# A delta-rule attention and expert kernel in a new line: joins on four quadrants, loads paced by products, first expert slots from 12 tiles

## The chip, the cores and the metric

One Trainium2 chip, one of its cores. The time is the device time of one execution in microseconds (us). The kernel before takes 500.79 us, the median of three runs (498.42 to 501.11). The change is large, so what a comparison can tell apart is far below what is at stake.

## The reference

Two parts. First a recurrence with a delta rule over 768 positions, for 4 batches of 8 heads with 48 columns; then a layer of 8 experts, of which each of the 3072 tokens takes one.

```python
k_n = k / (norm(k) + 1e-6); state = zeros(B, H, D, D)
for t in range(S):
    y[t]  = q[t] @ state
    v_old = state^T k_n[t]
    state = state + beta[t] * outer(k_n[t], v[t] - v_old)
x = y as [3072, 384]                       # token x (head, column)
logits = x @ w_gate + modality_bias[modality_id]
e = argmax(logits); gate = softmax(logits)[e]
out = gate * (relu(x @ w1[e]) @ w2[e])     # D 384, F 1024
```

## The kernel before

The recurrence is cut into 12 chunks of 64 positions. Inside a chunk the rule is a triangular system: the Gram matrix of the keys (`g`, function `gram`), scaled by beta, has to be inverted for every head. The 12 chunks are inverted in six sets of two, set 0 and 1 first. The inverse of a 64 x 64 triangle is put together: VectorE (DVE) solves small diagonal triangles column by column (`sub0_0` to `sub0_14`, lines 265 to 271, 16 x 16 for sets 0 and 1; `subx`, 32 x 32 for the others), and TensorE (PE) joins them. For sets 0 and 1 the joins of 16 to 32 are `jy`, `ya`, `jx`, `r1` (lines 289 to 302), one of each for each step i of 0 to 7: `jy` multiplies with the Gram blocks, `ya` scales the result, `jx` multiplies with the other triangle, `r1` adds it in. `wt`, `mva`, `mvb`, `mt` then lay the triangles out as R and its transpose RTB. The joins of 32 to 64 are `y1`, `ys`, `r`, `rc` (lines 375 to 389), for all 24 steps. For sets 2 to 5 the inverses travel through DRAM: `gd` writes Gram blocks, `la` reads them as rows, `rd` and `re` write the solved blocks and their transposes (made by `rt`), `rl` reads them into R and RTB.

The recurrence then runs in 24 steps i, two for a chunk (the two halves of the batch-head pairs, which alternate): `ks` (keys by state, PE), `rh` (DVE), `z` (inverse by right-hand side, PE), `zt` (eviction), `ds` (state update, PE), `sb` (eviction of the state), and beside them `pg`/`pe` (masked query-key products), `qs` and `pz` (the output y), `xo` (its eviction), `xd` (its store), `xt`/`xs` (transposes for the router) and, for each four steps, `lg`/`le`/`lt` (logits). All of it is a list of named tasks (`Plan`); the string `ORDER` (lines 28 to 49) gives their sequence, and each engine works its tasks in that sequence. SP issues the loads: `kqk`/`kq`/`ke` (keys and queries), `kv`, and it is one queue in order. `FILL` (lines 51 and 52) puts 33 matmuls of 128 x 128 by 128 columns, whose results nobody reads, ahead of named tasks (line 496).

When the logits of the first `C.tA` = 16 tiles of 128 tokens are there, `part_a` (tasks `pa`) fills the first `C.SA` = 2 slots of 512 tokens of one expert each. Their tokens are gathered (`xg`), transposed (`xp`), split into a high and a low part (`xh`, `xl`), and the first 4 of 8 blocks of the first slot's first product (`la_0` to `la_3`, three pieces each) are tasks of the attention plan. `part_b` does the same for all other tokens when the last logits are there. Behind the plan come the rest of the units (5 of 512 tokens, 2 of 256, one of at most 32), layer 1 at line 835 and layer 2 at line 926, and `out` is written by indirect scatters from GpSimd (POOL, line 930), in an order that the framework's scheduler makes.

## Time and profile before

| | us |
|---|---|
| median of three runs (lowest, highest) | 500.79 (498.42, 501.11) |
| the profiled execution | 503.82 |
| its span, first to last instruction | 502.0 |
| PE busy in it | 454.1 (90%) |
| DVE busy | 322.0 (64%) |
| ACT (ScalarE) busy | 215.0 (43%) |
| POOL busy | 132.9 (26%) |
| mean granted clock of PE | 0.908 of full |

How to read it: the shares are means over stages that differ. The first 85 us hold the Gram products, the first solver and the joins; the recurrence's steps run from there to about 260 us, with the solver of the later sets beside them; the experts take the rest. A matmul of float32 operands shows as two records of PE, so that 8 matmuls are 16 records. The granted clock is given as a share of 2.4 GHz; 0.50 is 1.2 GHz. "Idle before" a row is the time for which the engine stood still ahead of it, with what ended it; `issue` means that the profile shows no reason.

### The profile page before, as it was taken

To read this page: it belongs to the slowest core of one execution; us is meant where nothing else is said; L and a number is where in the kernel's file an instruction comes from. 1 tells how busy PE (TensorE), PEld (TensorE's weight loads), DVE (VectorE), ACT (ScalarE), POOL (GpSimd) and SP (SyncE) were. 2 spreads that over 40 slices of the span, in tenths; PEclk is the share of its full clock that TensorE was granted. 3 is DMA by queue.
4 is the path that set the end of the run, shared out by engine and by line. 5 is a ranking of instruction groups with operands and counts; after the bars stand their busy time and mean duration, and the time that the engine had idled before them with its cause. 6 is when DMAs were issued, how large, how long until landed. Compare 5 with 4: busy or idle time off the path is not lost. (4 is left out here: it accounts for less than half of the span.)

```text
span 502.0 us, 15898 instructions
## 1 busy us (share of the span) xinstructions
PE 454.1 (90%) x6661; PEld 405.2 (81%) x6661; DVE 322.0 (64%) x716; ACT 215.0 (43%) x471; POOL 132.9 (26%) x179
## 2 busy tenths in 40 slices
PE   6566999899899798998979999996999999999994
PEld 6456998787788687888768888895889889899983
DVE  3897798687789666786476887634345355345720
ACT  3623745786366351562454325213333334324520
POOL 9000613953633411101401012046103212001111
PEclk9555555999999998999898999998999999999998
DMA  8465503579477775876355516235415525239600
GB/s 291 167 142 154 172 3 89 140 190 320 133 196 191 191 228 152 231 194 181 114 172 186 194 63 190 63 108 187 140 55 166 181 73 183 80 101 359 187 20 34
DMA packets 81264, 78.07 MB, mean 156 GB/s; under 512 B 48009, under 2 KB 71568, under 8 KB 79904
## 3 DMA queue, kind: packets, MB, share of 16 engines
q1 hardware_dynamic: 78048, 67.49, 45.5%
q0 software_dynamic: 3136, 9.49, 5.6%
q8 instruction: 54, 0.88, 0.7%
q14 instruction: 26, 0.21, 0.1%
HBM read 62.27 MB, written 14.73 MB: 153 GB/s over the span
## 5 line engine op out<-in xcount | busy, mean ns | idle before, releaser
L926 PE MATMUL opb<-w2hb,h 128*128 128x384 f32 x192 | 53.0, 341 | 0.5 <-DVE oob L929 0.5
L841 DVE SCALAR_TENSOR_TENSOR h<-hpb,h 128x512 fp32r<-128x512 f32 x24 | 16.6, 692 | 44.1 <-ACT h L839 44.1
L835 PE MATMUL hpb<-xh,w1xb 128*128 128x512 f32 x144 | 41.9, 403 | 0.0
L926 PEld LDWEIGHTS opb<-w2hb,h 128*128 128x128 f32 x192 | 34.8, 188 | 1.8 <-DVE oob L929 1.0
L839 ACT ACTIVATE h<-hpb 128x512 fp32r<-128x512 f32 x24 | 14.3, 598 | 51.2 <-PE hpb L835 51.2
L926 PE MATMUL opa<-w2ha,h 128*128 128x384 f32 x128 | 34.6, 341 | 0.0
L332 POOL TENSOR_TENSOR tmx<-T,A 128x168 f32<-128x168 f32 (+13 forms) x27 | 20.5, 759 | 46.7 <-DVE T L333 45.3
L926 PE MATMUL opb<-w2lb,h 128*128 128x384 f32 x96 | 32.5, 338 | 0.0
L835 PEld LDWEIGHTS hpb<-xh,w1xb 128*128 128x128 f32 x144 | 27.4, 193 | 4.9
L416 DVE TENSOR_TENSOR RHS<-vv,ks 64x384 f32<-64x384 f32 x44 | 24.3, 552 | 6.5 <-PE ks L414 5.1
L930 POOL DMA_INDIRECT out_dram<-oob,sidxb x12 | 12.3, 1027 | 57.4 <-DVE oob L929 22.5
L178 PE MATMUL gp<-ke 48*64 48x64 f32 x576 | 17.7, 293 | 10.1 <-issue 4.5
L25 ACT COPY Sb<-S 48x192 f32<-48x192 f32 x58 | 18.1, 313 | 20.3 <-PE S L426 10.1
L795 POOL DMA_INDIRECT xgb<-xd,gidxb x12 | 12.5, 1045 | 49.2 <-DVE sidxb L707 24.0
L178 PEld LDWEIGHTS gp<-ke 48*64 48x64 f32 x576 | 15.6, 199 | 12.1 <-issue 7.7
L391 POOL TENSOR_TENSOR vv<-vv,RR 128x384 f32<-128x384 f32 x15 | 12.3, 836 | 48.8 <-DMA vv<-in_kv_dram 33.5
L926 PEld LDWEIGHTS opa<-w2ha,h 128*128 128x128 f32 x128 | 23.2, 188 | 0.8
L437 PE MATMUL y<-ZT,pb 128*64 128x96 f32 x384 | 23.1, 268 | 0.7 <-DVE ZT L26 0.5
L178 PE MATMUL gp<-kqr 48*64 48x64 f32 x896 | 18.2, 231 | 5.1 <-ACT gk L25 2.9
L333 POOL TENSOR_TENSOR T<-T,tmx 128x168 f32<-128x168 f32 (+13 forms) x27 | 22.1, 817 | 2.1
L414 PE MATMUL ks<-Sb,kqr 112*64 112x96 f32 x352 | 20.5, 255 | 1.9 <-issue 1.0
L25 ACT COPY R<-A 32x128 f32<-32x128 f32 x60 | 17.7, 296 | 10.2 <-DVE A L302 6.4
(340 smaller groups left out, 1169.9 us busy)
## 6 DMA issues: line engine op xcount, KB each, us to landing
kqr<-in_kq_dram SPq DMA_DIRECT2D x10, 1024.0 KB, 7.0
ke<-in_kq_dram SPq DMA_DIRECT2D x10, 512.0 KB
vv<-in_kv_dram SPq DMA_DIRECT2D x12, 384.0 KB, 5.4
xd<-xo SPq DMA_DIRECT2D x24, 192.0 KB, 2.8
w1rb<-in_moe_w_dram SPq DMA_DIRECT2D x12, 384.0 KB
w2rb<-in_moe_w_dram SPq DMA_DIRECT2D x12, 384.0 KB, 3.2
kk<-in_kv_dram SPq DMA_DIRECT2D x11, 384.0 KB, 6.5
w1ra<-in_moe_w_dram SPq DMA_DIRECT2D x8, 384.0 KB
```

Source lines behind the costliest of these rows:

```text
L25: if n=="scalar": nc.scalar.copy(o,i)
L178: s.I[f"g{c}"]=mm(t[p][64*h:64*h+64,64*(4*g+j):64*(4*g+j)+64],l,s.KQ[c][u:u+48,g,x,1] if a else l,start=True,stop=True)
L332: E[s.e].tensor_tensor(o,T[:,:,lo:lo+na,c:c+1].to_broadcast([128,n,na,nb]),X[:,:,c:c+1,c+1:32].to_broadcast([128,n,na,nb]),ALU.mult)
L333: x=T[:,:,lo:lo+na,c+1:32]; E[s.e].tensor_tensor(x,x,o,ALU.subtract)
L414: for p in range(2): mm(s.ks[i][64*p:64*p+64,:,j,:],s.KQ[c][:,g,4*p+j,0],hc(s.Sb[g][:,4*p+j,:]),start=True,stop=True)
L416: c,g=divmod(i,2); b=64*p; V.tensor_tensor(s.RHS[g][b:b+64,:,48*p:48*p+48].rearrange("q (h j) c -> q h j c",h=2),s.KV[c,1][b:b+64,g],s.ks[ ...
L437: for p in range(2): mm(s.y[i][64*p:64*p+64,:,j,:],s.PB[i//2][:,8*(i%2)+4*p+j],hc(s.ZT[i%2][:,4*p+j,:]),start=(i<2 and j==0),stop=True,ski ...
L795: s.nc.gpsimd.indirect_dma_start(xg,None,S["x"],bass.IndirectOffsetOnAxis(ap=S["gidx"][:,S["c0"]+t:S["c0"]+t+1].bitcast(U32),axis=0))
L835: if n in ks: mm=s.nc.tensor.matmul(hp[:,v,:],w[:,k,fs],x[:,k,0:T],start=(n==0),stop=(n==8))
L839: if k==0: s.nc.scalar.activation(hh,hp,AF.Relu)
L841: s.nc.vector.scalar_tensor_tensor(hl,hp,0.0,hh.bitcast(F32),ALU.max,ALU.subtract)
L926: mm=nc.tensor.matmul(op,h[:,f%nf,ts_],w[:,f%2,:],start=(n==0),stop=(n==23)); n+=1
```

## The change

The plan, its tasks and its order are replaced by those of a later line of the same kernel.

- **Joins.** `jy` and `jx` of steps 0 to 7 write to two PSUM banks, and four consecutive matmuls go to the four 64 x 64 quadrants of the array, not to the two on the diagonal. `wx` lays out the second operand for that. `y1` and `r` use 32 x 32 tiles for steps 0 to 7, and 64 x 64 quadrants with half of `r`'s matmuls for the others. R is laid out by whole-width copies (`mva`, `mvb`); RTB, `mt`, `rt` and `re` are gone, a transpose by DVE (`wt`) and, for steps 8 to 23, a copy `rq` are there instead.
- **Diagonal blocks of sets 0 and 1** come into D by masked whole-width instructions (`da`, `dc`), not by 32-partition copies; `norm` is split so that the part that only later steps need (`nr0`) is a task of its own; `fin0` is halved.
- **Fillers.** `FILL` is gone. In its place stand tasks `hf7` to `hf14` (2 x 128 columns, each waiting for one solver step), `hg0`, `hg1` (3 x 128) and `hx0` to `hx19` (2 x 128, no wait).
- **Loads.** `kq` and `kv` are loaded in halves and without the empty partitions 112 to 127. Each load of the kinds kq, ke, kv, wq, wr, la and rd and each store xd waits, by a semaphore, for the PE instruction that precedes it in the order.
- **Routing.** `C.tA` is 12; `part_a` starts when three groups of logits are there. `wq3`, `wr0`, `wr1` (a fourth block of w1 and two of w2) are loaded within the plan.
- **PSUM** banks are fixed tiles that the plan hands out itself. The scatters go to four disjoint views of `out`. In the last layer 2 all matmuls of a tile come behind those of the tile before (`fl` = 0).

The new ORDER sequences 1007 tasks (916 before). The core of the diff:

```diff
-    fl=4; tA=16; TA=512; SA=2; SB=3; SC=2; SE=1; FE=32; A1=2; A2=4; wr=4; xgb=4; w_q="sync"; wlp=(); wlq=(0,1,2,3)
+    fl=0; tA=12; TA=512; SA=2; SB=3; SC=2; SE=1; FE=32; A1=2; A2=4; wr=4; xgb=4; w_q="sync"; wlp=(); wlq=(0,1,2,3)
...
-            add(f"kq{c}","SP",.9,lambda c=c: gate("g3",lambda: kq(c,slice(1024,2048))),[f"kqk{c}","g3"],mb=.39)
+            add(f"kq{c}_1","SP",.4,lambda c=c: gate("g3",lambda: kq(c,slice(1024,2048))),[f"kqk{c}","g3"],mb=.52)
...
+                            p,h=(e,f) if a else (f,e); u=64*(h^p); x=4*p+j; l=s.KQ[c][u:u+48,g,x,0] if a else s.KE[c][u:u+48,g,x]
...
-        def dc(c,p):
+        def dx(c,h): x=16*h+8*(c%2); return s.D[:,c//2,x:x+8],s.gp[c][h].rearrange("q (x t) -> q x t",x=8)
+        def da(c,h): d,g=dx(c,h); mul(d,g[:,:,32:64],s.hm[:,1:2])
+        def dc(c,h): d,g=dx(c,h); V.scalar_tensor_tensor(d,g[:,:,0:32],s.hm[:,0:1],d,ALU.mult,ALU.add)
...
+        def idle(n,k=None):
+            def f(): mm(s.bk["y"][:,0:128*n],s.ident,s.ident.unsqueeze(1).to_broadcast([128,n,128]),start=False,stop=True,skip_group_check=True)
+            gate(k,f) if k else f()
+        fy=["gf1","gf5"]; fills=[f"hf{c}" for c in range(7,15)]+["hg0","hg1"]+[f"hx{n}" for n in range(20)]
+        for c in range(7,15): add(f"hf{c}","PE",.85,lambda c=c: idle(2,f"sub0_{c}"),[f"sub0_{c}",*fy])
+        for n,k in enumerate(("fin0_0","ft0")): add(f"hg{n}","PE",1.3,lambda k=k: idle(3,k),[k,*fy])
+        for n in range(20): add(f"hx{n}","PE",.43,lambda: idle(2),fy)
...
+                jt=lambda i: s.JO[(0,1,0,1,2,2,2,2)[i]]
                 def jy(i):
-                    if i%2==0: s.jo[i]=s.jo[i+1]=s.bank(f"jo{i}",("z","ks")[i//2]) if i<4 else s.mo(f"jo{i}")
+                    s.jo[i]=jt(i)
                     for j in range(4):
-                        for p in range(2):
-                            for h in range(2): q=64*h; x=4*p+j; o=256*(i%2)+32*x; mm(s.jo[i][q:q+64,o:o+32],s.GK[i][q:q+64,x],s.W1b[i//4][q:q+64,16*p+4*(i%4)+j],start=True,stop=True)
+                        for h in range(2):
+                            for p in range(2): q=64*p; mm(s.jo[i][p][64*(p^h):64*(p^h)+64,32*j:32*j+32],s.GK[i][q:q+64,2*j+h],s.W1b[i//4][q:q+64,16*h+4*(i%4)+j],start=True,stop=True)
...
+                                k=p^h; q=64*k; n=4*(i%4)+j; w=s.Wx[i//4][q:q+64,n] if h else s.W0[i//4][q:q+64,n]
+                                mm(s.jo[i][k][64*p:64*p+64,16*j:16*j+16],s.ya[q:q+64,i%2,p,j],w,start=True,stop=True)
...
+        def rq(i):
+            r=s.R[i%4].rearrange("q (j h) t -> q j h t",h=2)[:,:,:,32:64]
+            for p in range(2): b=64*p; cp(s.e,r[b:b+32,:,1],r[b+32:b+64,:,0])
...
+            t=s.pa.tile([128,8,32],F32,name=f"Wt{i}",tag="Wt",bufs=3); s.nc.vector.transpose(t,s.R[i%4][:,:,0:32]); s.Wt[i]=t.rearrange("q (j h) t -> q j h t",h=2)
...
+        end=plan.chain("pa",lambda dry: (R.mute() if dry else R).part_a(*(((Mute(),)*3,)+(Mute(),)*4 if dry else (s.places,s.sea,s.prt(),s.mo,tp))),["lt2","y1_11","rk","rk3"],prio=900)
...
+            if s.pe and t["eng"]=="SP" and t["mb"]>.1 and t["name"][:2] in ("kq","ke","kv","wq","wr","la","rd","xd"):
+                i=next(i for i in new if "DMA" in type(i).__name__); s.tc.add_manual_dep(i,s.pe.name,mybir.DependencyInfo(mybir.DependencyClass.Sync,mybir.DependencyReason.DATA),reason="pace")
+            if t["eng"]=="PE" and new: s.pe=new[-1]
...
+        s.tc=tc; s.nc=tc.nc; s.outs=dram_disjoint_views(out,4); s.ident=ident
+        s.n+=1; return s.outs[s.n%4]
-            sc=nc.gpsimd.indirect_dma_start(s.out,bass.IndirectOffsetOnAxis(ap=sidx[:,c:c+1].bitcast(U32),axis=0),oo,None,bounds_check=3071,oob_is_err=False)
+            sc=nc.gpsimd.indirect_dma_start(s.to(),bass.IndirectOffsetOnAxis(ap=sidx[:,c:c+1].bitcast(U32),axis=0),oo,None,bounds_check=3071,oob_is_err=False)
...
```

The order of PE's tasks about the joins, after:

```
g1 g0 g3 g2 g4 g5 pg0 hx5 hx0 hx15 hx8 hx7 g6 scl1 g7 hx17 hx1 hf8 hx4 hf12 hx14 g8 hx9 hx12
hg0 hx16 jy0 jy1 hf7 jx0 hx6 jx1 hf14 jy2 scl0 hg1 hf10 jy4 jx2 hx10 y1_0 hx11 jy3 jx4 hx13 r0
hx19 jy5 jx3 hf13 hf11 scl2 jx5 hx18 hf9 jy6 hx2 y1_1 jx6 z0 r1 hx3 jy7 ds0 y1_2 jx7 qs0 z1 pz0
g10 r2 ds1 ks2 qs1 y1_3 g9 pz1 r3 z2
```

and before:

```
g1 g0 g2 g3 g4 pg0 scl1 scl0 g5 g6 g7 g8 jy0 jy2 jy3 jx0 jy1 jx2 jx1 jy4 y1_0 jx3 r0 jx4 jy5 jy6
scl2 jy7 jx5 z0 jx6 jx7 y1_1 qs0 r1 ds0 g10 pz0 ks2 z1 qs1 g9 y1_2 g11 r2 ds1 pz1 y1_3 z2
```

(FILL adds 3 matmuls ahead of pz0, 4 ahead of ks2, 3 ahead of y1_2 and 6 ahead of g11, and 17 more behind z2.) At the end of the plan, after: `... z22 pg11 r23 ks23 lg4 qs22 la_0_0 la_0_1 xt21 la_0_2 la_1_0 la_1_1 pz22 la_1_2 z23 la_2_0 qs23 la_2_1 la_2_2 pz23 la_3_0 xt22 la_3_1 xt23 la_3_2 lg5`; before: `... z23 xp3 lg4 pz23 xt21 xt22 xt23 la_0_0 ... la_3_2 lg5`.

## Rows read from the trace of the kernel before

**Rows 1.** Page, part 2: busy tenths in 40 slices of 12.55 us
```profile
PE   6566999899899798998979999996999999999994
...
PEclk9555555999999998999898999998999999999998
...
DMA  8465503579477775876355516235415525239600
```

**Rows 2.** Windows of 10 us: PE, PEld, DVE, ACT, POOL busy, PEclk, DMA share, GB/s
```profile
50.00:60.00 10.00, 10.00 (x200) 9.66 (x197) 7.40 (x17) 7.01 (x23) 6.77 (x12) 0.50 0.60 168
...
60.00:70.00 10.00, 10.00 (x182) 9.83 (x182) 8.49 (x23) 7.58 (x25) 2.65 (x5) 0.50 0.13 49
...
80.00:90.00 10.00, 9.92 (x167) 8.66 (x160) 7.71 (x12) 4.63 (x14) 2.42 (x4) 0.71 0.53 152
```

**Rows 3.** Timeline of PE, 0:95 (start us, us, engine line op out<-in xcount)
```profile
28.43 1.97 PE L178 MATMUL gp<-ke 48*64 48x64 f32 x60 [0.77 <-DVE pb L187]
...
41.61 5.33 PE L293 MATMUL jo<-w1b,gk 64*64 64x32 f32 x96 [3.38 <-DVE w1b L139]
...
58.98 1.06 PE L386 MATMUL lv<-R,ys 32*32 32x32 f32 x32
```

**Rows 4.** Timeline of PE from 80 us on: fillers (L496), products, Gram products
```profile
80.47 1.65 PE L496 MATMUL S<-ident 128*128 128x128 f32 x6
...
83.53 2.08 PE L496 MATMUL S<-ident 128*128 128x128 f32 x8
...
86.36 0.83 PE L420 MATMUL z<-RHS,R 128*64 128x96 f32 x16
...
89.65 1.60 PE L496 MATMUL S<-ident 128*128 128x128 f32 x12
...
96.20 0.88 PE L420 MATMUL z<-RHS,R 128*64 128x96 f32 x16
...
97.67 0.69 PE L386 MATMUL lv<-R,ys 32*32 32x32 f32 x32
...
101.75 1.16 PE L178 MATMUL gp<-kqr 48*64 48x64 f32 x64
...
104.46 0.49 PE L496 MATMUL S<-ident 128*128 128x128 f32 x2
...
104.88 0.88 PE L437 MATMUL y<-ZT,pb 128*64 128x96 f32 x16
```

**Rows 5.** Timeline of DVE, 0:50
```profile
8.06 1.72 DVE L26 COPY D<-gp 32x256 f32<-32x256 f32 x4 [5.81 <-PE gp L178]
...
16.71 0.48 DVE L234 MEMSET S<- 128x512 f32 x1 [0.85 <-ACT gk L25]
...
25.24 0.22 DVE L269 TENSOR_TENSOR tm<-T,A 128x60 f32<-128x60 f32 x1
...
37.96 1.23 DVE L274 TENSOR_TENSOR T<-T,t 128x1024 f32<-128x1024 f32 x1
```

**Rows 6.** Groups by line and form (xcount | busy us, mean ns | idle before)
```profile
L187 DVE TENSOR_TENSOR pb<-gp,cst 128x256 f32<-128x256 f32 x48 | 17.3, 417 | 3.3 <-PE gp L178 3.0
```

**Rows 7.** Timeline of PE: idle before a row, in brackets
```profile
14.68 1.86 PE L178 MATMUL gp<-ke 48*64 48x64 f32 x57 [4.46 <-issue]
...
165.62 0.88 PE L414 MATMUL ks<-Sb,kqr 112*64 112x96 f32 x16 [0.87 <-DMA kqr<-in_kq_dram]
...
173.12 0.25 PE L386 MATMUL lv<-R,ys 32*32 32x32 f32 x5 [2.84 <-issue]
```

**Rows 8.** Timeline of PE: last z, last piece la_3 of the first expert
```profile
256.42 0.83 PE L420 MATMUL z<-RHS,R 128*64 128x96 f32 x16
...
273.99 0.86 PE L835 MATMUL hp<-xh,w1xa 128*128 128x512 f32 x3
```

**Rows 9.** Page, part 6: KB each, median us from issue to landing
```profile
kqr<-in_kq_dram SPq DMA_DIRECT2D x10, 1024.0 KB, 7.0
```

**Rows 10.** Timeline of POOL at the end: the last scatter
```profile
496.72 0.98 POOL L930 DMA_INDIRECT out_dram<-ooc,sidxb  x1 [2.40 <-DMA out_dram<-ooc,sidxb]
```

More of the change, by code (lines that the diff above doesn't have):

```diff
@@ L306, in mv @@
-                def mv(i,p):
-                    W=w0(s.Wn[i//4],i)[:,p]; Rv=s.R[i%4].rearrange("q (j h) t -> q j h t",h=2)
-                    for h in range(2):
-                        for b in (1,0):
-                            o=64*p+32*b; q=64*h+32*b; cp(s.e,Rv[o:o+32,:,h,32*b:32*b+32],W[q:q+32])
-                MV=dict(ACT=(1.25,0),DVE=(1.0,1),POOL=(1.6,1))
-                def mt(i):
-                    for h in range(2): q=64*h; cp(s.e,s.RTB[i%2][q:q+32,:,32*h:32*h+32],s.Wt[i][q:q+32])
@@ L577, in tasks @@
         if i==3:
[L578 to L579 removed]
+            p.add(f"lg{u}","PE",.7,lg,[f"xs{4*u+j}" for j in range(4)]+["rk0"],prio=c+2,take=dict(mo=1))
+            p.add(f"le{u}","ACT",.27,le,[f"lg{u}",f"lt{u-1}" if u else None],prio=c+2,give=dict(mo=1))
             p.add(f"lt{u}","DVE",.35,lt,[f"le{u}"],prio=c+2)
@@ L967, in tile_kernel @@
     with after(PE_,A.load.ins):
-        for l,q in [(1,3)]+[(2,q) for q in range(4)]: X.load(S,l,q)
+        for q in (2,3): X.load(S,2,q)
         for q in (2,3): X.split(S["W"][1],q)
```

367 lines of the change are left out of this document (202 added, 165 removed).

## Prediction

> **What bounds the kernel now.** I read the page's slices first. TensorE (PE) is busy nine tenths or more in most slices, while its granted clock stands at half in slices 2 to 7 and at full before and after [rows 1]. So there are two kernels: up to about 85 us one at 1.2 GHz, after it one at 2.4 GHz that PE fills. The 10 us windows say what the slow stretch is: from 50 to 70 us PE is busy 10.00 of 10 and VectorE (DVE) 7.4 to 8.5, and the clock is 0.50 all the same; it comes back inside 80:90 [rows 2]. The timeline of PE gives the content: from 41.61 us on, the joins (jy, jx) of the first eight steps, 16 groups of 32 matmul records. Ninety-six records take 5.33 us, 56 ns each, although each is only 64 x 64 by 32 columns [rows 3]. A Gram product of the same clock, whose four matmuls in a row go to four different quadrants, needs 1.97 us for 60 records, 33 ns each [rows 3]. Joins before use only the two diagonal quadrants. The clock rises after the filler matmuls of 128 x 128 at 80.47 and 83.53; the second product of the recurrence (z1) starts at 86.36, still at the foot of the rise, and z2 at 96.20 [rows 4].
>
> From z2 to the last z (256.42) it is 160 us for 21 steps, with PE rarely idle: the recurrence is held by PE's own stream [rows 1, 8]. Then come the experts; their slices of PE are nines almost to the end [rows 1].
>
> **The change part by part.** The sum is made on the profiled execution (503.82 us, its span 502.0); the median of the timed runs is 500.79, so 3 us go off at the end.
>
> *Up to the first join.* DVE sets this stretch: it starts at 8.06 and reaches the first solver step at 25.24, 17.2 us with one idle gap of 0.85 [rows 5]. Four groups of quarter copies at 1.72 (one is shown) are 6.9; in their place come 12 masked instructions of 128 x 256 on DVE (4 da, 8 dc), like the masks of pb at 417 ns [rows 6], 5.0. One more eviction costs some 0.6, the two memsets of 0.48 go behind r1_3, and the idle gap, a wait for ScalarE (ACT), should go as ACT copies less: 1.9 - 0.6 + 1.0 + 0.8 = 3.1. Splitting fin0 (1.23) brings the first half's transposes 0.6 forward [rows 5]. So the first join starts near 38 instead of 41.61; bounds: nothing (a new wait for a Gram product) and 4.
>
> *Joins on quadrants, and the clock.* The 512 join records at 56 ns are 28.4 us of PE. On four quadrants they should run at the Gram price: 33 ns at half clock (16.9), or 18 ns at full, from 1.16 us for 64 records [rows 4], 9.3. The price of the records is certain to lie between 56 and 18; I take 18 because of the fillers. The change takes out 33 fillers of 128 columns, all behind the joins, and puts 20 (hx) and 8 (hf) of 256 columns and 2 (hg) of 384 ahead of and between them. Five hx in a row follow pg0, where PE otherwise waits for masks and evictions: they are hidden there, and they are as dense as the two groups of fillers before which the clock was half and after which it was full [rows 4]. Between first join and z1, 15 fillers lie on the path. At full clock twelve filler records take 1.60 us (at 89.65) [rows 4], a filler of two records 0.27 and one of 256 columns 0.53; a filler alone took 0.42 from start to start, 0.15 more than its share of a run (104.46 to 104.88) [rows 4]. So 14 x 0.68 + 0.95 = 10.5. Add five groups y1 and r at 0.69, z0 and ds0 at 0.85 each at most [rows 4], a small selection: 5.4. From first join to z1: 9.3 + 10.5 + 5.4 = 25, so z1 at 63 and not 86.36. DVE's list from the first join to z0 holds 17 steps; by the same steps of before I estimate 17 us, so it runs beside PE's 22. From z1 to z2 nine fillers (2.4 us) go, which leaves 7 to 8 of 9.8: z2 near 71, **25 us earlier**. If the clock stayed low: rival 1.
>
> Here a rule of the Trainium skill speaks against the fillers: "TensorEngine Tiling (Array Packing)", Key Properties, has it that changing the tiling mode drains the engine, and every filler between joins changes it twice. The trace agrees in kind, with the 0.15 above, which the sum holds already; without it z1 would come 2.1 us sooner.
>
> *Small joins of the later steps, transfers.* y1 and r of steps 8 to 23 go to 64 x 64 quadrants, r with half the matmuls: between nothing and 0.3 us a step, 0 to 5; I take 3. On DVE a transpose (wtr) and a copy (rq, mostly on ACT and POOL) of some 0.45 each per step are added; ScalarE's rt and the RTB and RE transfers go. Seventeen fillers behind z2 go: 17 x 0.3 = 5. Against it, seven of the 12 pieces la of the first expert product, some 0.7 each, now lie before z23 (5), and DVE, whose 19 steps from z0 to z2 I estimate at 14 us by the same steps of before, is longer there than PE: 2 more. From z2 to z23 thus 159 instead of 160.
>
> *Loads behind products.* Every large load on SP now waits for the PE instruction ahead of it in the order. Behind such a wait stand the small transfers of the same queue: rl (inverse blocks), gd, xd; for these wait wtr, y1, and the xo ring. By the new order the half loads of kq are issued 5 to 19 us of PE work before their first user; a whole kqr load of twice the size landed in 7.0 [rows 9]. I cost it at nothing, hidden by those products; where cover is thin (kq7_0, kq9_1, kv10_0, 5 to 6 us) it may cost 1 to 2 us each. The gain side: PE's idle times that end for no shown reason, 4.46 and 2.84 us, and the one wait for kqr, 0.87 [rows 7], stand in or just behind slices whose transfer engines are at seven or eight tenths [rows 1]; with bursts spread they may shrink. That is 0 to 8; I take nothing.
>
> *From z23 to the last la piece.* Before: 256.42 to 274.8, 18.4 us [rows 8]. Left behind z23 in the new order are one qs and one pz group, two transposes and five la pieces of 0.7, with z23 itself 7 to 8 us: **10 us earlier**. This is what routing from 12 tiles buys: the expert's tokens are gathered before the last products. Its weights' loads move too (w1's fourth, w2's first two).
>
> *Experts and end.* The same units (five of 512 rows, two of 256, one small) at the same matmuls: nothing, give or take 5 for another interleaving. Scatters to four views of the output no longer wait for each other's landing; the last one waited 2.40 [rows 10]. Between nothing and that is to be had, by when the last eviction ends; I take 1.4.
>
> Sum: 25 + 1 + 10 + 1.4 = 37; 503.8 - 37.4 = 466.4 for a profiled run, 463 on the median's scale.
>
> **The rivals.** *1. The clock stays at 1.2 GHz through the joins.* For it: PE was busy 10.00 at 0.50 for 20 us and more [rows 2], so being busy is not enough. By the Trainium skill, "TensorE: Matmul & The Clock Gate", What's actually happening, activity releases the throttle; the trace doesn't bear that out for the joins. Against it: dense 128 x 128 work preceded the rise [rows 4]. Price: six filler records at half clock took 1.65 [rows 4], so 1.1 for 256 columns. Joins 16.9, fillers 17, the rest 9, and the first join near 47, as the ten fillers between g7 and it no longer fit: z1 at 89 or 90, 3 later than before. Risen then, 12 us of gain remain: about 489. *1b, the slower side:* no filler is left behind z1. If the clock rises only past some 110 us, the recurrence itself runs at half clock (a group of r took 1.06 against 0.69 at full [rows 3, 4]), 10 us lost in each 25, and the 12 us won elsewhere are gone: 505 or more.
>
> *2. DVE or SP becomes the bound of the recurrence.* DVE is at 7.7 to 8.5 of 10 where PE is at half clock [rows 2]; with PE twice as fast the solver's steps for sets 2 to 5 may end late, and y1_8 waits; or the paced loads come 1 us late in ten chunks. 10 to 15 us: 475.
>
> *3. The idle times without reason go too* and DVE keeps up: 8 to 15 us more gain, 450.
>
> *4. Quadrants don't overlap for 16 and 32 columns:* up to 38 ns more a record, 19 us: 482. The Gram rows speak against it.
>
> **How the numbers follow.** Forecast (455 to 474) 0.52; rival 3 0.13; rivals 2 and 4 0.17; rival 1 0.10; 1b 0.05, and loads late by over 3.8 us in each of ten chunks, which would also end above 500, 0.03. The range 444 to 486 leaves out rival 1, both slower cases and the edge of 3, two in ten. Faster by over 0.5% (about what a measurement here tells from no change): 0.90; within it 0.02; slower 0.08.
>
> **What would show it.** The clock's slices reach full by the third or fourth; the joins at about 18 ns a record; z1 near 63, z2 near 71, z23 near 230; la pieces ending near 237; no wait of a scatter for a scatter. Wrong, if PE waits for kqr or for R's transfers in each chunk, if DVE's slices stand at nine while PE's fall, or if the clock is still half at 60 us.

## The result, and the profile after

The changed kernel takes 486.42 us (median of 4 runs, 484.85 to 496.68) beside 500.95 for the one before (4 runs): a ratio of 0.970, 95% interval 0.964 to 0.977. It is faster, as forecast, but by 14.5 us where 37 were forecast, and the time lies just outside the range. Some executions of either kernel, here the one of 496.68, are over 1.5% above its fastest, and the ratios and their intervals leave them out. The profiled execution took 487.58 (span 485.7), 16.2 less than 503.82.

First the slices of the page after, the ones that answer to [rows 1].

```profile
PE   6689888967999899899997999995999999999994
...
PEclk9589997995999999798998999997999999999999
...
DMA  5776655754667566564677234156326325239601
```

A slice is 12.1 us. The clock is back by the fourth, where before it was half up to the seventh. But it falls again, to 7, 5 and 7 tenths in slices 7, 10 and 17, and PE has a 6 and a 7 in slices 9 and 10, where [rows 1] has nines. So the early part did most of what was forecast and something later gave part of it back. The windows cut at the products z tell where (columns as in [rows 2]): from z2, z5, z8, z17, z18 and z23 of the changed kernel, and to the end of the last la piece and of the span.

```profile
76.63:96.62 19.99, 19.79 (x541) 17.88 (x539) 14.98 (x28) 12.63 (x34) 9.30 (x10) 0.83 0.64 169
96.62:130.87 34.25, 27.26 (x664) 24.49 (x658) 28.00 (x50) 13.96 (x42) 21.12 (x27) 0.80 0.53 153
130.87:191.52 60.65, 56.81 (x1391) 50.30 (x1388) 50.10 (x120) 42.58 (x127) 32.84 (x40) 1.00 0.63 174
191.52:205.56 14.04, 11.19 (x198) 10.39 (x193) 6.77 (x20) 4.62 (x15) 2.20 (x4) 0.76 0.59 172
205.56:245.20 39.64, 38.32 (x722) 32.59 (x721) 27.09 (x64) 18.59 (x52) 6.11 (x7) 0.96 0.57 160
245.20:256.44 11.24, 11.24 (x91) 8.84 (x90) 7.50 (x11) 5.69 (x9) 0.00 (x0) 1.00 0.74 235
256.44:485.70 229.26, 212.75 (x1209) 191.65 (x1209) 117.74 (x250) 75.14 (x121) 48.21 (x45) 0.97 0.42 133
```

And three stretches of the kernel before, from its z5 to z8, z8 to z17 and z17 to z18:

```profile
120.98:142.00 21.02, 19.66 (x560) 17.09 (x559) 15.77 (x37) 11.02 (x30) 9.06 (x12) 1.00 0.61 153
142.00:212.10 70.10, 63.85 (x1580) 55.55 (x1574) 51.52 (x110) 33.78 (x82) 19.56 (x24) 0.95 0.74 207
212.10:217.25 5.15, 4.86 (x133) 4.42 (x129) 4.81 (x17) 3.01 (x9) 0.00 (x0) 1.00 0.36 68
```

| stretch | before, us | after, us | difference | forecast |
|---|---|---|---|---|
| start to z2 | 96.20 | 76.63 | -19.6 | -25 |
| z2 to z5 | 24.8 | 20.0 | -4.8 | |
| z5 to z8 | 21.0 | 34.3 | +13.2 | |
| z8 to z17 | 70.1 | 60.7 | -9.5 | |
| z17 to z18 | 5.2 | 14.0 | +8.9 | |
| z18 to z23 | 39.2 | 39.6 | +0.5 | z2 to z23: -1 |
| z23 to last la | 18.4 | 11.2 | -7.2 | -10 |
| last la to the end | 227.2 | 229.3 | +2.1 | -1.4 |

A stretch does not hold the same work in both kernels, since the order is another: TensorE has 664 records from z5 to z8 where it had 560, 198 where it had 133 from z17 to z18, and 1391 where it had 1580 from z8 to z17. So a part of these three differences is work that stands elsewhere now. The rest is waits and half clock.

Two stretches stand out. From z5 to z8 VectorE has 28.0 us of work where before it had 15.8, PE is idle for 7 of 34 us and the clock is 0.80. From z17 to z18 PE is idle for 2.9 of 14 and the clock is 0.76. The timeline of PE names the waits (columns as in [rows 3], the idle time before a row and its releaser in brackets):

```profile
38.56 0.24 PE L315 MATMUL z<-w1b,gk 64*64 64x32 f32 x1
...
39.05 0.65 PE L315 MATMUL S<-w1b,gk 64*64 64x32 f32 x32
...
64.62 0.88 PE L467 MATMUL z<-RHS,R 128*64 128x96 f32 x16
...
67.61 0.49 PE L484 MATMUL y<-ZT,pb 128*64 128x96 f32 x6 [1.62 <-issue]
...
76.14 0.56 PE L426 MATMUL gp<-R,ys 32*32 32x32 f32 x23 [1.36 <-issue]
76.63 0.88 PE L467 MATMUL z<-RHS,R 128*64 128x96 f32 x16
77.44 1.50 PE L188 MATMUL MO<-ke 48*64 48x64 f32 x64
...
112.59 1.55 PE L467 MATMUL z<-RHS,R 128*64 128x96 f32 x16 [5.44 <-DVE RHS L463]
...
193.51 0.88 PE L461 MATMUL ks<-Sb,kqr 112*64 112x96 f32 x16 [0.57 <-DMA kqr<-in_kq_dram]
...
197.32 1.85 PE L188 MATMUL MO<-kqr 48*64 48x64 f32 x64 [2.27 <-DMA kqr<-in_kq_dram]
```

First join (38.56), a join group at 20 ns a record (0.65 for 32; 56 in [rows 3]) and z1 (64.62; 86.36 in [rows 4]) are as forecast. Behind three of these waits, at 76.14, 112.59 and 197.32, the same instructions run at half clock for a while (1.50 and 1.85 for 64 Gram records, 1.16 at full [rows 4]); behind the one at 67.61 the clock stays up. What VectorE did ahead of and in the 5.44 us (same columns):

```profile
97.61 0.94 DVE L259 TENSOR_TENSOR tt<-tt,A 128x64 f32<-128x64 f32 x1
...
102.60 0.55 DVE L437 TENSOR_TENSOR vv<-vv,RR 128x384 f32<-128x384 f32 x1
103.07 2.35 DVE L269 TENSOR_TENSOR A<-A,t 128x1024 f32<-128x1024 f32 x2
105.34 1.42 DVE L356 TENSOR_TENSOR tmx<-T,A 128x216 f32<-128x216 f32 x1
106.79 1.31 DVE L357 TENSOR_TENSOR T<-T,tmx 128x216 f32<-128x216 f32 x1
...
109.56 0.56 DVE L463 TENSOR_TENSOR RHS<-vv,ks 64x384 f32<-64x384 f32 x1
```

Step 6's differences (L463) stand in its queue behind the scaling of the third set (L269) and the last steps of the second elimination (L356, L357). Before the change that elimination's last step was at 102.60 us, between z3 and z4; after, it is at 110.15, between z5 and z6: the recurrence had caught up with it.

VectorE's instructions also take longer there. The norm's 0.94 (L259) is 0.27 in the kernel before, where GpSimd did nothing at the time:

```profile
114.13 0.27 DVE L243 TENSOR_TENSOR tt<-tt,A 128x64 f32<-128x64 f32 x1
```

Five such instructions of the norm and the step of 1.42 and 1.31 make some 5 of the 12 us that VectorE has more, an estimate from the durations of the same forms beside an idle GpSimd. No run takes this part by itself.

### The profile page after: what moved, and what is told of

The parts are those of the page before. It is cut to its first block, busy times and chain, and to the rows that moved or that the text cites. A ratio compares the mean times of both kernels' runs of the same rounds, so it can differ in the third digit from the quotient of the medians.

```text
span 485.7 us, 15721 instructions
## 1 busy us (share of the span) xinstructions
PE 438.1 (90%) x6567; PEld 386.7 (80%) x6567; DVE 313.0 (64%) x684; ACT 206.4 (43%) x488; POOL 154.1 (32%) x197
## 4 chain that ended last, share of the span: by engine, by line
PE 68%; DVE 14%; DMA 7%; issue 4%; ACT 2%; POOL 2%; SPq 1%; another core or an unknown queue 1%; POOLq 0%; DVEq 0%; ACTq 0%
PE hpb L889 11%; PE opb L980 9%; PE opa L980 6%; PE hpa L889 5%; PE hpc L889 4%; PE opc L980 3%; PE MO L188 3%; PE z L467 3%; PE S L473 3%; PE ks L461 3%; PE y L481 2%; PE y L484 2%; DMA w1ra<-in_moe_w_dram 2%; DVE tmx L356 2%; DVE T L357 1%
## 5 line engine op out<-in xcount | busy, mean ns | idle before, releaser
L356 POOL TENSOR_TENSOR tmx<-T,A 128x440 f32<-128x440 f32 (+14 forms) x31 | 26.6, 859 | 32.8 <-DVE T L357 31.3
L980 PE MATMUL opb<-w2lb,h 128*128 128x384 f32 x96 | 32.3, 336 | 0.0
L26 ACT COPY Sb<-S 48x192 f32<-48x192 f32 x70 | 21.9, 313 | 19.9 <-PE S L473 14.2
L463 DVE TENSOR_TENSOR RHS<-vv,ks 64x384 f32<-64x384 f32 x44 | 24.2, 550 | 9.5 <-PE ks L461 8.6
L357 POOL TENSOR_TENSOR T<-T,tmx 128x440 f32<-128x440 f32 (+14 forms) x31 | 27.8, 896 | 2.4
L467 PE MATMUL z<-RHS,R 128*64 128x96 f32 x384 | 22.2, 261 | 5.6 <-DVE RHS L463 5.6
L188 PE MATMUL MO<-kqr 48*64 48x64 f32 x832 | 19.3, 245 | 6.9 <-DMA kqr<-in_kq_dram 4.7
L26 ACT COPY ZT<-z 64x384 f32<-64x384 f32 x35 | 16.5, 472 | 20.0 <-PE z L467 19.2
L26 ACT COPY R<-gp 32x128 f32<-32x128 f32 (+1 forms) x72 | 20.2, 280 | 9.7 <-PE gp L426 5.9
L467 PEld LDWEIGHTS z<-RHS,R 128*64 128x64 f32 x384 | 18.0, 144 | 7.4 <-DVE RHS L463 6.1
L188 PEld LDWEIGHTS MO<-kqr 48*64 48x64 f32 x832 | 16.8, 156 | 8.9 <-ACT gk L26 2.6
L461 PE MATMUL ks<-Sb,kqr 112*64 112x96 f32 x352 | 21.9, 266 | 1.6 <-ACT Sb L26 0.7
```

What stands on the lines that cost most here:

```text
L26: if n=="scalar": nc.scalar.copy(o,i)
L188: s.I[f"g{c}"]=mm(t[e][64*f:64*f+64,64*(4*g+j):64*(4*g+j)+64],l,s.KQ[c][u:u+48,g,x,1] if a else l,start=True,stop=True).ins
L356: E[s.e].tensor_tensor(o,T[:,:,lo:lo+na,c:c+1].to_broadcast([128,n,na,nb]),X[:,:,c:c+1,c+1:32].to_broadcast([128,n,na,nb]),ALU.mult)
L357: x=T[:,:,lo:lo+na,c+1:32]; E[s.e].tensor_tensor(x,x,o,ALU.subtract)
L461: for p in range(2): mm(s.ks[i][64*p:64*p+64,:,j,:],s.KQ[c][:,g,4*p+j,0],hc(s.Sb[g][:,4*p+j,:]),start=True,stop=True)
L463: c,g=divmod(i,2); b=64*p; V.tensor_tensor(s.RHS[g][b:b+64,:,48*p:48*p+48].rearrange("q (h j) c -> q h j c",h=2),s.KV[c,1][b:b+64,g],s.ks[ ...
```

## The experiments

Times are ratios to the kernel before on the same chip. The changed kernel was measured twice, 0.970 (0.964 to 0.977) and 0.964 (0.957 to 0.972), so differences of less than 0.7% between two measurements say nothing. Executions of the same instructions also differ: ten profiles of kernels whose TensorE instructions don't differ before z2 (one lacks steps of an elimination) have it at 76.6 to 81.4, mean 79.6, and the changed kernel's own is the earliest.

**The early stretch: quadrants, clock or loads?** Without the fillers:

```diff
-def f(): mm(s.bk["y"][:,0:128*n],s.ident,...)
+def f(): return
```

> The 30 filler products ahead of z of step 0 are left out (20 bare ones, 8 behind steps of the first elimination, 2 behind its end). Theory C (the early gain is mostly the clock that they bring back): the granted clock stays at 1.2 GHz from 24 us until z of step 1 or 2, a group of 32 join products takes 1.3 us instead of 0.65 and a group of 64 Gram products 1.97 instead of 1.16, z of step 2 comes 12 to 20 us later (89 to 97 instead of 76.6), the kernel takes 497 to 507. Rival Q (the quadrants carry the gain, and the joins wait for VectorE anyway): z of step 2 by 82, the kernel within 5 us of 486.

Measured: 0.977 (0.969 to 0.985), z2 at 80.0. The clock is half through the joins (windows of 10 us), yet in the timeline of PE a group of 32 takes 1.08, against 1.89 for the old form at that clock:

```profile
40.00:50.00 10.00, 9.02 (x300) 8.62 (x304) 8.47 (x17) 7.64 (x26) 5.53 (x9) 0.50 0.66 192
50.00:60.00 10.00, 5.88 (x192) 5.34 (x185) 7.91 (x22) 3.21 (x13) 7.54 (x11) 0.50 0.59 176
```

```profile
46.42 1.08 PE L315 MATMUL MO<-w1b,gk 64*64 64x32 f32 x32
...
54.76 1.08 PE L315 MATMUL MO<-w1b,gk 64*64 64x32 f32 x32 [2.60 <-DVE A L331]
```

Theory C fell, Q held: the gain does not need the fillers, and the quadrants shorten the joins without them. How much of the gain they carry no run shows, as none takes the quadrants away alone, and without the loads' tie (below) most of it goes with the quadrants in place. At half clock PE is busy only 5.9 of 10 from 50 to 60 and waits for VectorE, so the clock has little to add: nothing at z2 (the ten profiles have 79.6 in the mean), and in the time 0.7 to 1.3%, which the intervals don't tell from nothing.

The reverse, the clock without the quadrants, twice. The kernel before, with fillers ahead of and between its joins (task:count, the tasks by their names):

```diff
-FILL="444:3 ... 559:1"
+FILL="444:3 ... 559:1 g6:20 g8:10 jy0:12 jy2:4 jx0:6 jy1:4 jx2:4 jx1:4 jy4:4 jx3:4 jx4:4"
```

> The kernel before, its joins not on quadrants, with 76 more products of the identity with itself (128x128) on TensorE ahead of and between its Gram products and joins from 25 us on, as many as the changed kernel has there, 20 of them ahead of the 7th chunk's Gram product. Theory C (the clock is what the early gain needs: at 2.4 GHz the old joins take half as long): the granted clock is back at 2.4 GHz by 35 us and stays, 32 join products take 0.95 to 1 us instead of 1.9, z of step 1 comes at 68 to 76 instead of 86.4, and the kernel takes 483 to 492. Rival Q (the form of the joins carries it: products of 64 rows that don't run beside one another leave the clock low however busy TensorE is): the clock falls back to 1.2 GHz inside the joins, z of step 1 at 84 or later, the kernel at 498 or more.

Measured: 0.992 (0.983 to 1.001), z1 at 85.0. The clock held to 70, a group took 1.11, and the fillers between the groups (1.16 a piece) took the room. That decides nothing, so next only 26 of them, all ahead of the joins:

```diff
+FILL="444:3 ... 559:1 g6:16 g8:6 jy0:4"
```

> The kernel before with 26 more products of the identity only ahead of its joins (16 ahead of the 7th chunk's Gram product, 6 and 4 where TensorE waited 2.7 and 3.4 us before 36 and 42), none between them. In the run with 76 the clock stood at 2.4 GHz from 32 to 68, the old joins took 1.11 us a group of 32 instead of 1.9, and the products between them took the room back. Theory C (the clock alone gives the old joins what the new ones have): the first join group starts at 41 to 43, the clock holds through the joins, 16 groups take about 18 us instead of 30, z of step 1 comes at 70 to 77 instead of 86.4, and the kernel gains 8 to 15 us. Rival Q (without work between them the old joins let the clock fall, or VectorE's chain behind them takes the time): z of step 1 at 82 or later and the kernel within 4 us of before.

Measured: 0.989 (0.982 to 0.996), z1 at 81.1, between the two expectations. Windows and timeline of PE:

```profile
40.00:50.00 10.00, 7.99 (x233) 7.70 (x232) 8.97 (x20) 6.08 (x14) 3.21 (x8) 0.94 0.82 210
50.00:60.00 10.00, 10.00 (x200) 9.66 (x197) 8.40 (x22) 7.94 (x26) 7.07 (x11) 0.50 0.65 204
```

```profile
46.47 1.12 PE L293 MATMUL jo<-w1b,gk 64*64 64x32 f32 x32 [0.58 <-DVE A L302]
...
49.84 1.90 PE L293 MATMUL jo<-w1b,gk 64*64 64x32 f32 x32
```

The clock goes down within the old joins, with no gap between 46.47 and 49.84, and PE is busy 10.00 of 10 right behind at 0.50. So what Q expected is seen. Whether the joins or the idle time ahead of them (0.58 here, 1.43 before 41.90) brought the clock down is not shown, as the run with 76 fillers had filled both. As far as the clock holds, it is worth about 5 us (z1 at 81.1 instead of 86.4).

The loads without their tie to products:

```diff
-if s.pe and t["eng"]=="SP" and t["mb"]>.1 and ...:
+if False and t["eng"]=="SP" and t["mb"]>.1 and ...:
```

> The loads and the spills no longer wait for the TensorE instruction ahead of them in the order; every other dependency stands. Theory P (tying loads to products costs what its thin covers lose): the waits of 0.57 and 2.27 us for the second half of the 9th chunk's keys before 197 go, the half clock from 197 to 205 with them (about 3.5 us in L188, L745 and the steps there), and the kernel gains 4 to 7 us (479 to 482). The rival, that the loads set free collide with one another and the spills: the landing of a 448 KB load goes from 4.8 to 6 us or more, new waits for a DMA show up between 60 and 190, and the time is 486 or more.

Measured: 0.995 (0.990 to 0.999), 499.04 us: nearly all of the gain is gone, and not by the rival's late loads. The windows and two waits:

```profile
40.00:50.00 10.00, 7.47 (x204) 5.20 (x206) 6.93 (x20) 5.29 (x19) 2.98 (x5) 0.96 0.99 253
50.00:60.00 10.00, 7.34 (x157) 5.75 (x154) 1.65 (x3) 3.25 (x11) 7.04 (x8) 0.50 1.01 199
60.00:70.00 10.00, 10.00 (x160) 6.93 (x161) 4.77 (x18) 1.84 (x7) 5.09 (x9) 0.50 0.11 36
```

```profile
47.55 0.24 PE L315 MATMUL z<-w1b,gk 64*64 64x32 f32 x1 [2.53 <-issue]
...
56.20 0.31 PE L407 MATMUL gp<-Wt,gk 32*32 32x32 f32 x3 [2.66 <-issue]
```

Loads fill the DMA engines (0.99 and 1.01), PE stands still twice with no releaser, the second time inside one group of matmuls, VectorE does 1.65 us of work in 10, and the clock is half until 80; z2 comes at 90.0. The two waits are 5.2 us of the 10 to 13 by which z2 is later. Behind them the fillers run at half clock: from 47.5 us on 24 records of them take 12.9 us, in the changed kernel 18 take 5.8. Loads without the tie and without fillers were not tried. At the 9th chunk, on the other hand, the waits for keys are gone and z18 follows z17 after 8.0 us.

That points at traffic for the waits without a releaser. The changed kernel has one inside step 0's values (67.61), as have eight of the ten profiles, its own among them, 1.6 to 2.2 us at the same record. So its traffic there was cut:

```diff
+if c==2 and x.start==0: x=slice(0,16)        # kq
+w=16 if c==2 else 768; ... t[:,0:w] ...      # kv
```

> In the changed kernel the loads of the third chunk's keys and values (three transfers of 384 to 448 KB, issued at 61.7, 65.6 and 70.7) are cut to 16 columns each, so that these values are wrong; all instructions stay, and in their order. Theory F (TensorE's two waits without any releaser, 1.62 us inside the values' product of step 0 at 67.6 and 1.36 inside the product of R and ys at 76.1, are its instructions arriving late because data fills the DMA engines): both waits go below 0.5, no half clock follows between 70 and 82, z of step 2 follows z of step 0 after 12 to 14 us instead of 17.1 (17 to 19 in the other runs of the same instructions), and the kernel gains 2 to 5 us. Rival I (they arrive late whatever the data does): the first wait stays at 1.5 to 2.2 us at the same instruction, with the half clock behind it, and z of step 2 within 1 us of before.

Measured: 0.967 (0.956 to 0.979), so the time doesn't tell; the trace does.

```profile
70.00:80.00 10.00, 9.18 (x342) 8.11 (x332) 8.91 (x16) 6.57 (x18) 5.17 (x6) 1.00 0.31 61
```

```profile
68.26 1.14 PE L486 MATMUL y<-ZT,pb 128*64 128x96 f32 x16
...
76.61 0.56 PE L428 MATMUL gp<-R,ys 32*32 32x32 f32 x23 [0.54 <-issue]
```

The first wait is gone, the second is 0.54, no half clock follows, and z2 follows z0 after 14.2 us, where the ten need 15.0 to 19.8. That is within 0.2 us of what theory F expected. As two of the ten are without the first wait too, one profile makes F likely and no more; that the wait goes where traffic is put (the runs with loads moved, below) speaks for it as well.

**Steps 5 to 8.** Step 6's differences first:

```diff
-VectorE: n2 vs6 sc2 subx1_27 subx1_28 subx1_29 rh1_6 subx1_30 rs1_0 rh0_6 xo5 rs1_1 subx2_2 rh1_7 rh0_7
+VectorE: n2 vs6 rh1_6 rh0_6 sc2 subx1_27 subx1_28 subx1_29 subx1_30 rs1_0 xo5 rs1_1 subx2_2 rh1_7 rh0_7
```

> VectorE's two differences for step 6 (L463) stand right behind the product ks of step 6 in the order, ahead of the scaling of the second set (L269) and of two steps of the elimination. Theory S (the order on VectorE made TensorE wait 5.44 us before z of step 6, and the half clock behind it, z 1.55 instead of 0.88, ks 1.49, the values 1.99, is an echo of that wait): the wait goes to under 1 us, the clock stays at 2.4 GHz from 105 to 122, z of step 9 comes 9 to 10 us earlier (at about 125), and the whole kernel gains 6 to 10 us (476 to 480). Theory D (VectorE is full there, so whatever is put first only pushes the rest back): a wait of 3 to 5 us appears at one of the steps 7 to 10, and the kernel stays within 3 us of 486.

Measured: 0.973 (0.965 to 0.981). Theory S fell; D's forecast held, with a wait of 6.73 us for its 3 to 5: z6 came 5 us sooner and z7 1 us.

```profile
108.08 0.83 PE L469 MATMUL z<-RHS,R 128*64 128x96 f32 x16
...
118.01 1.55 PE L469 MATMUL z<-RHS,R 128*64 128x96 f32 x16 [6.73 <-DVE RHS L465]
```

Holding the clock instead, with fillers in the gap:

```diff
+if i==6:
+    for _ in range(22): mm(s.S[1][:,384:512],s.ident,s.ident,start=False,stop=True,...)
```

> 22 products of the identity with itself (128x128, 0.2 us each at 2.4 GHz) are put on TensorE ahead of z of step 6, where it waited 5.44 us; nothing else is changed. Theory S (the low clock is the echo of the wait): z of step 6 starts at about the same time (112.6, within 0.5), but takes 0.88 instead of 1.55, and the next eight groups lose their extra 4 to 4.5 us in sum; z of step 9 at about 130 instead of 134.3; the kernel gains 3 to 5 us. The rival, that the clock would have fallen there whatever TensorE did (or that the steps behind are paced by VectorE and not by TensorE): z of step 9 within 1 us of 134.3, the kernel within 1.5 us of 486.

Measured: 0.973 (0.967 to 0.980). The 22 products took 6.23 us, so z6 came 1 us later; it takes 0.88 at full clock, then y1 of step 8 waits 2.08 for VectorE, and z9 follows z5 after 38.1 us, 37.7 without. The half clock behind the wait costs next to nothing here: what it slowed would have waited.

A shorter second elimination, after and before (`if J==1 and 8<=c<20: return` as the first line of `sub`):

> Twelve of the 30 steps of the second elimination (columns 8 to 19, two instructions each) are left out of the changed kernel; nothing else. They take about 20 us of the 56 us between its first step (54.56) and its last (110.4). Theory V (after the change the recurrence arrives at step 6 before the second elimination is done, and from there z of step 8 waits for that elimination, its spill and its reload): the wait of 5.44 us before z of step 6 goes, the span from z of step 5 to z of step 8, 34.3 us now, falls to 21 to 25, and the kernel gains 7 to 13 us (473 to 479). Rival T (the recurrence is paced by TensorE's own work and clock from step 2 on): 34 us stay within 3, and the kernel within 3 us of 486.

> The same twelve steps of the second elimination left out of the kernel before. There its last step was at 103 us and z of step 8 at 142, with 21 us between z of step 5 and z of step 8. Theory V: the elimination was done well ahead of its use, so the kernel before gains little from a shorter one: 0 to 4 us (497 to 501), z of step 8 less than 4 us earlier against z of step 1. Rival (VectorE's work as such, whoever waits for it, costs time in both): the kernel before gains as much as the changed one does.

Measured: 0.974 (0.965 to 0.984) and 0.998 (0.994 to 1.002); z5 to z8 32.4 and 20.1 us. Theory V fell: with 12 steps less, z6 still waits 4.77 us, since the last four steps stand behind the third set's norm and scaling in VectorE's queue and come no sooner. So it is not the length of the elimination. The kernel before, with its slack, tells nothing apart then.

Its end sooner, by another order, with the norm and scaling behind step 7:

```diff
-POOL: subx1_25 subx1_26 vs7 ti2            VectorE: n2 vs6 sc2 subx1_27 ... subx1_30 rs1_0 ... rh0_7
+POOL: subx1_25 ... subx1_30 vs7 ti2        VectorE: vs6 rh1_6 rh0_6 rs1_0 rs1_1 ... rh0_7 n2 sc2
```

> In the changed kernel the last four steps of the second elimination go from VectorE to GpSimd, right behind the 26th, and its end (L368) stands ahead of the norm and scaling of the third set (L259 to L269), which move behind step 7's differences, as do the first steps of the third elimination; step 6's differences stand right behind their product. The whole computation is done. Theory V: the second elimination ends at about 105 instead of 110.4, no wait over 1.5 us is left before z of steps 6 and 7, z of step 8 comes 4 to 7 us earlier, and the kernel gains 3 to 7 us, if the third elimination, which then starts 8 us later, still ends ahead of step 16. Rival (it does not, or VectorE's queue is simply full): z of step 8 gains, z of step 16 doesn't, and the kernel stays within 2 us of 486.

Measured: 0.987 (0.979 to 0.995), worse. z6 comes without a wait; then PE waits 2.82 us for the norm (`scl5`, now just ahead of z7) and 5.51 for `pb`, and z8 follows z5 after 39.0, though VectorE has 22.0 us of work there and not 28.0.

Then VectorE relieved, with the next run as its measure (both have the 9th chunk's loads earlier, below):

```diff
-VectorE: ... sc2 subx1_27 ... subx1_30 rs1_0 ... rs1_1 subx2_2 rh1_7
+VectorE: ... sc2 rh1_6 rh0_6 rs1_0 ... subx2_2 rh1_7            POOL: subx1_25 ... subx1_30 vs7 ti2 rs1_1
```

> The changed kernel with the 9th chunk's loads behind the product of step 15, and with VectorE relieved between steps 5 and 8 of 6 to 7 us: the last four steps of the second elimination and the last multiplication of its second set (L368) go to GpSimd, and step 6's differences stand right behind their product; the norm and scaling of the third set stay where they were. The whole computation is done. Theory D (what VectorE has queued between steps 5 and 8 paces z of steps 6 to 8, whatever is put first): the wait of 5.4 us before z of step 6 and the 6.7 us that took its place before z of step 7 when only step 6 was put first are both under 2 us, z of step 8 follows z of step 5 after 27 to 30 us instead of 32 to 34, and the kernel gains 3 to 6 us on the one with the loads alone. Rival G (GpSimd becomes as late as VectorE was, since it must still fill the third set's matrices, and z of step 7 or 8 waits for its share): 32 to 34 us stay, no gain.

> The changed kernel with the 9th chunk's loads behind the product of step 15 and nothing else changed, again, as the measure for the run beside it: 0.960 to 0.969 of the kernel before, no wait for these loads, 5 to 6 us of wait before z of step 6.

Measured: 0.958 (0.953 to 0.964) and 0.968 (0.962 to 0.973): a gain by these ratios, but the medians of all their runs stand the other way (485.84 and 483.44), and z8 follows z5 after 32.4 us still; nine profiles with VectorE's order as it was, the changed kernel's among them, have 32.1 to 35.1. z6 no longer waits; z7 does, 5.78 us, while VectorE is idle:

```profile
110.24 0.55 DVE L27 COPY xo<-y 128x384 f32<-128x384 f32 x1
115.82 0.28 DVE L358 TENSOR_TENSOR tmx<-T,A 128x116 f32<-128x116 f32 x1 [5.03 <-POOL T L359]
...
116.45 1.12 DVE L465 TENSOR_TENSOR RHS<-vv,ks 64x384 f32<-64x384 f32 x2
```

Step 7's differences stood behind a step of the third elimination that waited for GpSimd. So theory D is too simple: an engine idle for 5 us isn't full. Two last orders move step 7's differences ahead of it, one on VectorE alone, one with the relief:

```diff
+e17: VectorE: n2 vs6 subx1_27 ... subx1_30 rs1_0 rh1_6 rh0_6 sc2 xo5 rh1_7 rh0_7 rs1_1 subx2_2 ... pe3_0
+e18: as e15, and rh1_7 rh0_7 ahead of subx2_2
```

> The changed kernel with loads placed as in the run with both load moves, and in VectorE's order between steps 5 and 8 only the positions changed: the last four steps of the second elimination and the first multiplication of its end (L368) stand ahead of the scaling of the third set (L269), step 6's and step 7's differences each right behind their product, the reloads of R ahead of one store. Nothing goes to another engine. Theory W (not VectorE's amount of work but what stands ahead in its queue sets this stretch: the differences behind elimination steps, and the second elimination's end, on which z of step 8 waits through its spill and reload, behind the third set's scaling): its end (the first L368) comes at 106 to 108 instead of 110.7, the waits before z of steps 6 and 7 are under 1.5 us each, z of step 8 follows z of step 5 after 27 to 30 us instead of 32 to 35, the kernel gains 4 to 7 us on the one with the loads alone: 0.945 to 0.955 of before. Theory D (the amount): the wait moves to z of step 8 or 9, 32 us or more stay, 0.958 to 0.965 of before.

> The run that relieved VectorE, with the differences of step 7 too right behind their product (there they stood behind a step of the third elimination that waited 5.03 us for GpSimd) and the loads placed as in the run with both load moves. Theory W: no wait over 1.5 us before z of steps 6 and 7, z of step 7 at most 5 us behind z of step 6; z of step 8 then waits for the second elimination's end, whose multiplication is no earlier than before (108.5), so that z of step 8 still follows z of step 5 after 30 to 32 us, and the kernel is at 0.952 to 0.96 of before. Theory D: as for the run beside it.

Measured: 0.960 (0.953 to 0.967) and 0.953 (0.947 to 0.959), the lowest of all. The same loads with VectorE's order as it was had 0.961 (0.956 to 0.965, below), so the first order shows no gain of its own, and the second 0.8% at most, with intervals that overlap. In the first, PE, then VectorE:

```profile
103.66 0.88 PE L469 MATMUL z<-RHS,R 128*64 128x96 f32 x16 [0.81 <-DVE RHS L465]
...
107.63 0.88 PE L469 MATMUL z<-RHS,R 128*64 128x96 f32 x16 [0.72 <-DVE RHS L465]
...
113.93 0.38 PE L486 MATMUL y<-ZT,pb 128*64 128x96 f32 x2 [4.09 <-DVE pb L201]
```

```profile
98.46 0.37 DVE L358 TENSOR_TENSOR tmx<-T,A 128x216 f32<-128x216 f32 x1
...
110.61 0.28 DVE L358 TENSOR_TENSOR tmx<-T,A 128x116 f32<-128x116 f32 x1 [1.98 <-POOL T L359]
```

The waits before z6 and z7 are gone, as theory W had it, and the next thing behind the third elimination is late instead: `pb` (L201). z8 follows z5 after 32.3 us once more, against W's 27 to 30; in the second, whose profiled execution took 492.15, after 35.4, with 4.87 us before `pb`. So W's waits went and its gain did not come; the wait moved on and the 32 us stayed, as theory D forecast, though VectorE is idle for 6 of the 32 us. Nor was it the second elimination's end: it comes 8.9 us behind z5 (101.22), not 14.1, and z8 is no sooner. So two things are shown: the waits of this stretch are the order of VectorE's queue (each moved when the order did, and VectorE idled behind GpSimd in the meantime), and neither the clock nor the elimination's length makes them. No order made the stretch shorter than the shortest with the order as it was (32.1): TensorE's idle time in it is 7.0 us in the changed kernel and 7.4 in the first of these two. What would bound z8 once no step of the recurrence stands behind an elimination step was not tried and stays open.

**Steps 17 and 18.** The 9th chunk's loads behind step 15's product:

```diff
-SP: ... rl19 rl18 kq9_0 rd2_1 kq9_1 xd15
+SP: ... kq9_0 kq9_1 xd13 kv9_1 kv8_0 rl19 rl18 rd2_1 xd15
```

> In the changed kernel the two halves of the 9th chunk's queries and keys are issued behind the product of Q and the state of step 15, ahead of ten other transfers on SP, instead of behind steps 16 and 17's work. Theory L (their late issue at 188.8 and 190.5 and a landing of 6.8 us made TensorE wait 0.57 and 2.27 us and then run at 1.2 GHz until 205): the waits go, z of step 18 follows z of step 17 after 7 to 9 us instead of 14.1, and the kernel gains 4 to 7 us (479 to 482). Rival (the first part of the routing, or the reloads of R that now stand behind these loads, take the place of the wait): z of step 18 gains under 2 us, the kernel within 2 us of 486.

Measured: 0.969 (0.961 to 0.977); 0.968 when run again (above). In the trace the stretch is as theory L had it:

```profile
192.43:200.40 7.97, 7.97 (x198) 7.39 (x193) 6.50 (x22) 4.02 (x13) 2.65 (x4) 1.00 0.54 148
```

z18 follows z17 after 8.0 us, at full clock, without an idle gap. So 6.1 of the 8.9 us were the waits and the half clock, and the other 2.8 are the 65 records more. The time, 484.48, misses the 479 to 482 of the expectation, and the two ratios lie between the changed kernel's two. A part of the 6.1 us is lost just ahead, as the rival had it: z17 follows z16 after 8.4 us, 9.8 when run again, where it was 7.1. In the repeated run TensorE waits 1.60 us for `kk`, a values' load that now stands behind the keys on SP. With the third chunk's load and the first spill moved too:

> The changed kernel, with the 9th chunk's loads behind the product of step 15 as before, and the third chunk's first load and the first spill of Gram products (256 KB) moved from ahead of z of step 1 to behind the 11th chunk's Gram product, so that the stretch in which TensorE waited 1.6 to 2.2 us for instructions has less traffic. The whole computation is done. If traffic is the cause there, the wait in step 0's values goes under 0.8 us, z of step 2 follows z of step 0 after 14 to 15.5 us, and with the 9th chunk's loads the kernel gains 4 to 9 us on the changed one on the same chip. If the traffic only moves (the spills then fill the stretch from 70 to 80), the second wait grows to 2 us or more and z of step 2 gains nothing; 2 to 5 us are left.

> The changed kernel itself, on the same chip as the others here, as the measure for them: 0.965 to 0.975 of the kernel before; its two waits without a releaser at the same instructions (inside step 0's values, inside the product of R and ys of step 3), 5 to 6 us of wait before z of step 6, 1.5 to 2.5 us for the 9th chunk's second load.

Measured: 0.961 (0.956 to 0.965) beside 0.964 (0.957 to 0.972) for the changed kernel. The wait in step 0's values went, and one of 1.70 us came at 75.40, inside the product ks of step 2, right behind the place where the load and the spill now stand. The two later runs with these loads have such a wait too (1.43 and 1.14 us ahead of z2). So the traffic most likely only moved, as the second half of the expectation had it.

**The scatters**, on one view again (`return s.outs[0]`):

> In the changed kernel all scatters to the output use one view again, so that one must have landed before the next is issued, as before the change. Theory (the four views are worth what the last scatter waited, 2.40 us on the 17th expert's last one, and little else): the last scatter waits 1 to 2.5 us again, and the kernel is 1 to 3 us slower than the changed one on the same chip. Rival (the scatters also held the expert stage up, a term that the prediction didn't have): 4 us slower or more. Rival (nothing: the last one comes late anyway): within 0.7 us.

Measured: 0.979 (0.973 to 0.986) beside that 0.964; the medians of all six runs are 492.69 and 490.02, 0.5% apart. By the ratio the first rival is right, by the medians the theory, so the time decides nothing. In the trace the end is the same: 6.50 us from the last product's end to the end of the span, 6.35 with four views (7.5 in the kernel before), and 228.4 against 229.3 from the last la piece on. But the profiled execution, 488.25, is the fastest of the six, so what the others lost was not seen. The term of 1.4 is not shown.

## Why the prediction was right and wrong

The sum was 37.4 us and the profiled executions are 16.2 apart. Of the 21 that are missing, 5.4 lie ahead of z2, 9.4 between z2 and z23, 2.8 between z23 and the last la piece, 3.5 behind it.

*Right:* the first join (38; 38.56), the price of a join record (18 ns at full clock, 33 at half; 20 and 34), and z1 (63; 64.62, and 66 to 71 in the other nine profiles).

*"From z1 to z2 nine fillers go, which leaves 7 to 8."* It took 12.0. Two waits without a releaser (1.62 and 1.36) are 3 us; the forecast knew such waits [rows 7] and took nothing for them. And by the new order pz0, ks2 and r3, 0.7 to 0.9 each, stand between z1 and z2, where y1_2 stood: more work that the forecast didn't count. In the other nine profiles z2 comes 1 to 5 us later still, so the first term, 25, measured 15 to 20.

*"Loads behind products: I cost it at nothing, hidden."* This is the largest error of mechanism. The tie is worth some 12 us (0.995 without, 0.970 with), all in the first 90 us: 5.2 of waits without a releaser, most likely since loads get in the way of TensorE's instructions, and behind them fillers at half clock. Without it the first term would have been 6. The gain side, "0 to 8, I take nothing", was the place where this stood.

*The clock.* The 25 were argued from fillers that bring back the clock, and rival 1 priced their failure at 26 us. They are worth nothing at z2 and 6 in the time at most: the quadrants alone nearly halve a group at the same clock (1.89 to 1.08), and then VectorE is what the joins wait for. The 490.64 measured without fillers is no proof of rival 1's 489: its sum has 17 us of fillers at half clock, and without them z1 was at 70, not at 89. Where the fillers did run at half clock, in the run without the tie, they took 17.2 us from 38 on. That the joins were PE's 28.4 us before was right (28.5 in its trace); that PE's own work and clock would remain their bound was not.

*"From z2 to z23 thus 159 instead of 160."* It took 168.6, the term that failed by most, 9 us. The step that failed is "the recurrence is held by PE's own stream": PE is idle for 15.2 us of it (11.9 before), and busy for 153.4 (148.4) with some 145 records fewer, as it runs at half clock for a part. Rival 2 was at work from z5 to z8: step 6's differences stand behind the elimination in VectorE's queue (5.44 us). The sum had no term for that; its 2 us for DVE were for the steps from z0 to z2. From z17 to z18 it was a thin cover, kq9_1, priced at 1 to 2: 2.8 us of waits and the half clock that follows, 6.1 together. The two stretches are 13.2 and 8.9 us longer and the others from z2 to z23 14 shorter, but both figures hold work that changed its place; some 5 of the 13.2 are such work, by an estimate (TensorE is busy 24.9 us there in the order on VectorE alone, at a clock of 0.95, and 19.7 before).

*"10 us earlier"* from z23 to the last la piece: 7.2. *Experts:* 2.1 later instead of 1.4 earlier, by the last group of the router (PE waits 2.60 for it, now behind the last la piece) and a handover between experts that waits 5.79 for its tokens, where before it was 4.33.

## What to carry to other kernels

When a change moves one engine's work forward by 20 us, go through what every other engine has in its queue at the new time, in order, not how busy it is on the average: a step that waits at the head of an in-order queue holds back all that stands behind it. Moving one instruction ahead only showed the next one here, and no order tried made the stretch shorter. When two kernels are compared between two events, count the work between them first: an order that moves work makes one stretch look slow and another fast. And before crediting a gain to a clock or to a layout, ask which engine bounds the stretch once both are there.
